# A shift filter in 32-row TensorE tiles, its gating in 1024-wide passes, and exchanges of 512 KB, in a kernel whose instruction order is written out

## Chip, cores, metric

One core of one Trainium2 chip. The metric is device microseconds of one execution. Of the many chips that were used, each comparison uses one: a changed kernel and the kernel before run in turn on the same chip. (e1 to e4 ran on one chip, e5 to e8, e17 and e18 on a second, e9 to e15 on a third, e16 on a fourth; runs of different chips are compared only by their ratios to the kernel before.) A run counts as slow, and is left out of the ratios, when it is over 1.5% above the fastest of the same kernel.

## The reference, cut

Two blocks on 2048 rows of 512 channels, in bf16. The change lies in the first.

```
k_shift = sum over t in 0..3 of k_pad[:, t:t+S, :] * shift_k[:, 3-t]     # a causal filter of 4 taps, per channel
kv = k_shift * v                                                          # "gating"
y  = irfft2(rfft2(kv padded to 2S) * rfft2(ssm_k padded to 2S))[:S]       # a long convolution per channel
out1 = q * (y + kv * ssm_D)
# ... then block B: layer norm, w1, gelu, w2, layer norm, w3 (512 to 1792), gelu, w4
```

## The kernel before: the parts that matter

Every piece of work is a numbered task; one string, ORDER, lists all of them in the order in which they are emitted. A word is a task, its engine (P TensorE, V VectorE, A ScalarE, G GpSimd, S the DMA queue on SyncE, M one merged ScalarE eviction for two tasks) and its PSUM banks. Each engine runs its own words in that order; waits between engines follow from the data. So a late task holds up all words behind it on its engine.

```python
ORDER = """
002S 023V 021P7 033V 022P 051P01 003S 052A 055P23 ...   # [cut: 791 words]
"""
    def emit(self):
        for word in ORDER.split():
            t, slots, i = self.t[int(word[:3])], [int(c) for c in word[4:]], 0
            ...                                         # [cut]
            t["fn"](word[3], t["got"].get("ps", slots))

    def shift(g, c):                     # filter of 512 rows (g) and 128 channels (c), into one bank
        s, b4 = divmod(g, 2)
        def f(e, sl):
            o = ps[:, sl[0], :]
            for i, d in enumerate((0, 1, 2, 3, -1, -2, -3)):
                j0, j1 = max(0, -d), min(3, 3 - d)
                ...                      # [cut: row block bb, offset x]
                nc.tensor.matmul(o[:, (d + j0) * P:(d + j1 + 1) * P], lhsT=kT[s][c][:, bb, x:x + P],
                                 rhs=diag[:, c, j0:j1 + 1, :].rearrange("p j x -> p (j x)"), start=(i == 0), stop=(i == 6))
        return f

    for g in range(2):                   # exchange between the two steps of a transform, 256 KB each
        for kl in range(4):
            nc.sync.dma_start(z2[sig][g:P:2, kl, :, :], z1[sig][kl:P:4, 2 * g:2 * g + 2, :, :])   # [a task ("X", sig, g, kl)]
```

The names in the profile: r_k is k, r_dg the diagonals with the taps (a per-channel product done as a matmul with a diagonal matrix), r_kv the gated product, r_x and r_y the results of a transform's first step, r_f and r_a the same data after the exchange, r_p the products of spectra, r_vs the inverse transform's first result.

Of the kernel before, what the change touches and what calls it, by code (L numbers as in the profile page):

```python
# [9 lines left out]
P = 128  # L10
# [3 lines left out]
DC = D // P  # L14
FC = F // P
NB = 8
# [15 lines left out]
002S 023V 021P7 033V 022P 051P01 003S 052A 055P23 056A 057P45 005S 025V 029V 001S 000S 024V 053P01 034G 041V 058A 047P23 049P67 048A 008S 028G 007S  # L32
027V 050A 083P50 032V 089P4 091P71 097P6 009S 084V 010S 031G 054A 042V 043A 006S 026G 030A 095P5 004S 014S 059P01 060A 061P23 038V 090V 035G 062A
093P4 015S 087P1 098V 096V 011S 036V 037A 039V 040A 085P6 092V 094V 111P23 020S 112A 064S 088V 086V 107P01 108V 109P45 110A 045G 113P67 114A 012S
103P23 105P01 066S 106A 104V 099P45 100V 101P67 102A 013S 019S 063S 340V 175P31 176V 335G 067S 018S 071P0145 073A 179P7 343V 338V 180V 072A 339V 068S
342V 119S 120S 074P2345 076A 075A 177P6 178V 115S 123P0145 124A 125V 046G 135V0 116S 126P6723 128A 127A 065S 117S 121S 129P0145 131A 130A 136V1
137P23670 139V2 016S 138V3 145V0 118S 140P 144V1 148V2 183P50 184V 069S 147V3 141A 077P0123 341V 142A 146P45671 149P 017S 337V 079A 154V0 070S 078A
153V1 122S 132P0123 134V 150M 151A 133A 143S 080P4567 155P01230 157V2 156V3 158P 336V 081A 162V0 082A 163V1 165V2 166V3 181P5 152S 185P4 344G 182V
160A 159A 161S 164P23671 167P 168A 169V 170S 189P1 186V 187P0 195P23 044A 190V 188V 332S 197P45 345G 346G 347G0 198V 196A 191P67 192A 193P01 194A
203P23 204V 205P45 199P67 200V 206A 350G1 171P10 351V 201P23 202A 229S 227S 348V 349A 356G1 353G0 352A 172P76 173P54 239P01 357V 358A 230S 231P23 240A  # L40
232A 354V 228S 362V1 363V 364A 359V0 371G 355V 331S 214S 241P67 242A 207S 372G 373V 368G1 374V0 360V 377V1 233P01 174P43 234A 369V 243P67 244A 361A
375P20 376V 213S 209S 384G 385G 365G0 378P5 379V 245P01 235P67 246A 386V 387V0 208S 397G 398G 237P23 238A 380P5 390V1 236A 370A 366V 367A 410G 210S
388P11 391P0 211S 212S 251S 392V 382P4 383A 389V 248S 252S 381A 215P2367 399V 400V0 395P1 403V1 401P00 404P4 216V 250S 405V 217A 268V0 402A 393P5 394A
396A 267V1 270V2 221P2367 223A 411G 406P4 412G 413G0 408P5 258P0167 407A 249S 222V 259V 416G1 414P40 260V 409A 423P5 417P3 415A 418A 424V 425A 427P4
428V 429A 253S 247S 261P0123 263V 447G 421P7 422A 419P6 420A 271V3 262V 224P2345 226A 225A 435P7 436V 431P6 432V 334S 255P0145 256V 443P7 333S 437A
433A 448G 449G 450G0 451P60 444V 257V 452A 218P0123 220A 219A 453G1 454P6 455V 439P7 254S 269P23450 476G 272P 477G 478G 480A0 479V1 456P60 457A 466P1
481S 274V0 273V1 275P 276V2 467A 277V3 278P 280A 440V 282V0 279A 264P0167 283V1 464P5 465A 468P4 265V 445A 284P01231 286V2 285V3 441A 287P 266V 632G
288V0 482S 483S1 469A 289V1 292V2 291V3 484P50 496P4 497A 485A 492P7 493A 290P 293P 294A 488P7 434V 633G 634G 490P6 430V 491A 494P5 281S 489A 298V0
297V1 301V2 486P4 299P01670 300V3 304V0 495A 636G0 638S 302P 487A 501P5 635V1 295A 296S 303V1 306V2 307V3 305P 308P 309A 438V 502V0 503S 498P4 310A
312V0 313V1 314P01231 315V2 316V3 317P 499V1 318V0 462P7 319V1 321V2 504S 322V3 508V 458P6 459A 509V 507S 515V 514V 505S 511V 463A 506S 512V 513V  # L50
460P5 461A 320P 323P 324M 325A 637S 470P7 311S 510V 473P6 516V 517G 500S 426V 471V0 326S 474V1 518V 522V0 519A1 327P75 523V 528G0 524A 520V 521A
328P64 529V 534A0 525V1 329P32 330P51 639S0 640P70 644P4 650P0 526V 531V1 530A 527A 535V 543G 544G 545V 549V0 546V1 645A 651A 642P6 643A 641A 646P4
647A 547P20 532V 536V 533A 556G 652P0 557G 558V 559A1 540G0 472S 548V 550P4 551V 560V0 537V1 538V 648P7 649A 653A 541V 561S 562S 542A 568G 569G 570V
571V1 539A 552P6 573S 572V0 554P4 555A 574S 654P7 553A 592P6 593V 596P5 580G 581G 597V 582G 584V0 583A1 657P4 563S0 566P6 567A 442V 564P5 565A 598V
594V 660V 661G 662V 664G0 655V0 575S1 578P3 579A 663V1 576P6 577A 608P5 609V 585S 586S 587S0 475S 588P7 589A 590P5 612P6 666S 665S 613V 667S0 591A
616P5 617V 620P7 621V 622A 604P6 610A 614V 688G 668P50 670P7 678P3 605V 680P6 671A 599V 618A 716V 669A 689G 690V 679A 692V0 694S 691V1 693S 600P7 601V
603V 602A 672P5 673A 674P3 675A 717G 718G 719V0 720V1 681A 695S1 722S 676P7 677A 624P5 625V 626A 628P6 623V 685P7 595V 606V 744V 745G 746G 696P50
708P3 709A 682P2 627V 706P3 721S 629V 631V 723S0 700P6 701A 630A 446V 747G0 749S 611V 702P1 703A 619V 683V1 684S 724P20 732P6 707A 697A 726P3 728P5
704P1 727A 615V 748V1 750S 772G 773G 774G 776A0 658V1 778S 698P4 725A 733A 730P0 656S 736P6 751S1 699A 734P4 731A 705A 710P3 713P2 752P10 729A 775V1
735A 777S 779S0 764P0 711V0 756P3 757A 753A 780P50 781A 788P4 784P3 785A 789A 754P1 782P5 783A 659S 714V1 715S 790P4 786P3 792P5 737A 738P6 686V1 791A  # L60
687S 787A 793A 797P7 794P5 760P4 761A 758P3 795V1 796S 712S 759A 607V 762P5 763A 798V1 799S 741P4 739V0 740S 765A 755A 766P5 742V1 743S 767V0 768S
769P7 770V1 771S
# [39 lines left out]
def body(ctx, tc, fx, kt, q, v, sd, w1, w2, w3, w4, out):  # L102
# [69 lines left out]
    diag = r_dg[:].rearrange("p (c j x) -> p c j x", c=DC, j=4)  # L172
# [7 lines left out]
    hbt = ct("hbt", 2, D)  # L180
    junk = {"A": ct("junka", D, dt=mybir.dt.uint8), "V": ct("junkv", D, dt=mybir.dt.uint8)}
# [57 lines left out]
    make_identity(nc, ident[:])  # L239
    ui, us = ti[0][:, 0:512], ti[1]  # L240
# [10 lines left out]
    for o, terms in enumerate((((4, 16), (2, 8), (0, 4), (1, 2), (5, 1)), ((6, 64), (7, 1)), ((3, -1024), (7, 3072)), ((3, 3072),),  # L251
                               ((5, 4), (6, 8), (0, 128), (1, 256), (2, 512), (3, 1024), (4, 2048)), ((5, 64), (0, 16), (1, 32), (7, 1)),
                               ((3, -3072), (7, 3072)), ((4, 2), (2, 1)))):
        for b, w in terms:
            pool.memset(wf[:, o, b:b + 1], float(w))
# [45 lines left out]
    add("wend", {PEc: 0.01}, lambda e, sl: None, drop=[("warm", 0)])  # L301
# [4 lines left out]

    def dg(c):
        def f(e, sl):
            for j in range(4):
                sc = sskf[:, 4 * c + j:4 * c + j + 1]  # L310
                if e == GP:
                    pool.tensor_scalar(out=diag[:, c, j, :], in0=ident[:], scalar1=sc, scalar2=0.0, op0=MUL, op1=ADD)
# [536 lines left out]
```

## Time and profile before

| | before |
|---|---|
| time, median of 3 | 213.88 us (213.87 to 214.77) |
| span of the profiled run, mean granted clock | 211.8 us, 1.00 |
| matmuls and PE busy | 2388, 197.7 us (93%) |
| VectorE, ScalarE busy | 145.5 us, 126.6 us |
| shift filter on PE | 112 matmuls, 15.3 us |
| rear, from the second half's product transform to the end | 168.4 us |

### The profile page before, as it was taken

The page shows a single profiled execution, that of the slowest core. Times are in us where ns is not written, and L with a number is a line of the kernel's source. Part 1 is how long each engine was busy: PE and PEld are TensorE (multiplying, and loading weights), DVE is VectorE, ACT ScalarE, POOL GpSimd, SP SyncE. Part 2 cuts the span into 40 slices and gives each one's busy share as a digit, 9 for nine tenths or more (in the row PEclk, how much of TensorE's full clock was granted, in tenths as well). Part 3 has the DMA queues.
Part 4 walks back from the last instruction along what each step waited for, and adds up shares of the span by engine and source line. Part 5 has one row for each costly group of instructions (what it writes and reads, how often), then busy time and mean ns, then how long its engine had stood idle before and what let it go on. Part 6 is the DMA issues. An engine that isn't in the chain of part 4 may idle for free.

```text
span 211.8 us, 5915 instructions
## 1 busy us (share of the span) xinstructions
PE 197.7 (93%) x2388; PEld 118.7 (56%) x2388; DVE 145.5 (69%) x322; ACT 126.6 (60%) x205; POOL 67.5 (32%) x171
## 2 busy tenths in 40 slices
PE   7999866998899998999999999989999999999993
PEld 5554322543375546674654784747657866864641
DVE  7699999999978999969789994627695102100421
ACT  4979899798998796672261875335622740540500
POOL 7534000765956452570003774202153200000000
PEclk9999999999999999999999999999999999999999
DMA  6999893388949952503576028470262252000111
GB/s 213 333 384 362 342 314 153 128 265 260 407 183 313 421 215 55 152 19 124 125 251 159 3 51 127 89 148 11 53 148 55 47 130 69 28 0 0 64 60 50
DMA packets 31772, 33.42 MB, mean 158 GB/s; under 512 B 22529, under 2 KB 24578, under 8 KB 31490
## 3 DMA queue, kind: packets, MB, share of 16 engines
q1 hardware_dynamic: 31746, 33.06, 49.3%
q8 instruction: 18, 0.29, 0.6%
q14 instruction: 8, 0.07, 0.1%
HBM read 13.13 MB, written 4.72 MB: 84 GB/s over the span
## 4 chain that ended last, share of the span: by engine, by line
PE 60%; ACT 14%; DMA 12%; issue 5%; SPq 4%; DVE 3%; POOL 0%; DVEq 0%; ACTq 0%
PE ps L774 20%; PE ps L786 20%; PE ps L723 6%; PE ps L694 6%; ACT r_x L265 4%; DMA r_k<-in_kt_dram 3%; ACT r_y L265 3%; DMA r_q<-in_q_dram 3%; DMA r_f<-r_x 2%; PE ps L494 2%; SPq L276 2%; PE ps L513 2%; SPq L413 2%; PE ps L421 2%; DMA dlb<-r_k 2%
## 5 line engine op out<-in xcount | busy, mean ns | idle before, releaser
L774 PE MATMUL ps<-r_dg,r_k 128*128 128x256 bf16 x448 | 51.2, 273 | 0.8 <-ACT r_vs L265 0.6
L774 PEld LDWEIGHTS <-r_k 128*128 128x128 bf16 x448 | 43.3, 98 | 8.9 <-issue 2.1
L788 DVE TENSOR_TENSOR ob<-ps,r_a 128x512 bf16<-128x512 f32 x5 | 3.5, 692 | 22.9 <-PE ps L786 21.5
L786 PE MATMUL ps<-w4s,r_kv 128*128 128x512 bf16 x84 | 19.0, 379 | 0.0
L778 ACT ACTIVATE r_f<-ps 128x512 bf16<-128x512 f32 x16 | 9.2, 595 | 15.0 <-PE ps L774 15.0
L265 ACT CAST r_x<-ps 128x1024 bf16<-128x1024 f32 x16 | 15.2, 1021 | 2.3 <-PE ps L397 2.3
L694 PE MATMUL ps<-hnT,r_v 128*128 128x256 bf16 x128 | 15.5, 273 | 1.0 <-DVE r_q L726 0.9
L778 ACT ACTIVATE r_kv<-ps 128x512 bf16<-128x512 f32 x21 | 11.7, 594 | 7.0 <-PE ps L774 7.0
L494 PE MATMUL ps<-r_p,ttab 32*32 32x512 bf16 x768 | 15.2, 378 | 0.7 <-ACT r_a L265 0.3
L723 PE MATMUL ps<-r_v,r_h 128*128 128x512 bf16 x64 | 15.5, 379 | 0.0
L450 PE MATMUL ps<-r_dg,r_k 128*128 128x256 bf16 (+3 forms) x112 | 15.3, 288 | 0.0
L778 ACT ACTIVATE r_y<-ps 128x512 bf16<-128x512 f32 x12 | 6.9, 597 | 13.9 <-PE ps L774 13.9
L786 PE MATMUL ps<-w4s,r_f 128*128 128x512 bf16 x64 | 15.1, 379 | 0.0
L694 PEld LDWEIGHTS <-r_v 128*128 128x128 bf16 x128 | 12.1, 98 | 4.8 <-issue 1.5
L265 ACT CAST r_vs<-ps 128x1024 bf16<-128x1024 f32 x11 | 10.9, 1039 | 5.8 <-PE ps L494 4.7
L265 ACT CAST r_f<-ps 128x1024 bf16<-128x1024 f32 x14 | 13.6, 1028 | 0.7 <-PE ps L421 0.7
L397 PEld LDWEIGHTS <-f 128*32 128x32 bf16 x256 | 6.9, 100 | 11.8 <-issue 6.9
L450 PEld LDWEIGHTS <-r_k 128*128 128x128 bf16 x112 | 9.3, 98 | 7.4 <-issue 2.7
L698 ACT ACTIVATE r_h<-ps 128x512 bf16<-128x512 f32 x16 | 9.1, 611 | 7.1 <-PE ps L694 7.1
L786 PEld LDWEIGHTS <-r_kv 128*128 128x128 bf16 x84 | 8.1, 98 | 9.3 <-issue 0.2
L494 PEld LDWEIGHTS <-ttab 32*32 32x32 bf16 x768 | 8.2, 88 | 7.4 <-issue 5.3
L458 DVE TENSOR_TENSOR r_kv<-ps,r_v 128x512 bf16<-128x512 f32 x16 | 10.3, 680 | 2.0 <-DMA r_v<-in_v_dram 2.0
(177 smaller groups left out, 364.8 us busy)
## 6 DMA issues: line engine op xcount, KB each, us to landing
r_x<-r_vs SPq DMA_DIRECT2D x8, 512.0 KB, 3.4
r_k<-in_kt_dram SPq DMA_DIRECT2D x8, 259.0 KB, 6.6
r_v<-in_v_dram SPq DMA_DIRECT2D x4, 512.0 KB, 6.2
r_q<-in_q_dram SPq DMA_DIRECT2D x8, 256.0 KB, 5.2
r_f<-r_x SPq DMA_DIRECT2D x8, 256.0 KB, 5.5
r_a<-r_y SPq DMA_DIRECT2D x8, 256.0 KB, 3.2
r_f<-r_y SPq DMA_DIRECT2D x8, 256.0 KB, 6.1
r_y<-r_x SPq DMA_DIRECT2D x8, 256.0 KB, 3.6
```

The lines of the kernel that those rows point to most:

```text
L265: (act.copy if e in "AM" else on[e].tensor_copy)(o, i)
L276: add(name, {SP: 0.47 if size < 400 else 0.6}, lambda e, s: nc.sync.dma_start(dst, src), deps, size=size)
L397: nc.tensor.matmul(ps[32 * j:32 * j + 32, sl[hh], :], lhsT=f1t[:, 4 * t + 2 * hp + hh, :], rhs=src(2 * b + b0), start=True, stop=True)
L450: nc.tensor.matmul(o[:, (d + j0) * P:(d + j1 + 1) * P], lhsT=kT[s][c][:, bb, x:x + P], rhs=diag[:, c, j0:j1 + 1, :].rearrange("p j x -> p ...
L458: vec.tensor_tensor(out=kvs[:, got(("K", g, 0), "kv")[0], :, c * P:(c + 1) * P], in0=ps[:, got(("K", g, c))[0], :].rearrange("p (b x) -> p ...
L494: nc.tensor.matmul(ps[c:c + 32, bk[h], :], lhsT=ttab[32 * h:32 * h + 32, 2 * kl + t, 2 if x else xx, 32 * b0:32 * b0 + 32], rhs=prs[32 * h ...
L694: nc.tensor.matmul(ps[:, sl[0], j * 256:(j + 1) * 256], lhsT=w1s[:, k, m * P:(m + 1) * P], rhs=hnT[:, k_, k, :], start=(k == 0), stop=(k = ...
L698: act.activation(h1T[:, 2 * h:2 * h + 2, 2 * p:2 * p + 2, 1 + P * s:1 + P * s + P], ps[:, got(("W", s, p, h))[0], :].rearrange("p (j b x) ...
L723: nc.tensor.matmul(ps[:, sl[0], :], lhsT=h1T[:, m, bb, x:x + P], rhs=w2s[:, m, :], start=(m == 0), stop=(m == DC - 1))
L774: nc.tensor.matmul(ps[:, sl[0], j * 256:(j + 1) * 256], lhsT=w3s[:, k, fc * P:(fc + 1) * P], rhs=lnT[:, k_, k, :], start=(k == 0), stop=(k ...
L778: act.activation(gb(gi, 2 * fp, 2), ps[:, got(("M", s, p, fp))[0], :].rearrange("p (j x) -> p j x", j=2), ACT.Gelu_apprx_tanh)
L786: nc.tensor.matmul(ps[:, sl[0], :], lhsT=gb(gi, fc)[:, 0, (b % 2) * P:(b % 2 + 1) * P], rhs=w4s[:, fc, :], start=(fc == 0), stop=(fc == FC ...
```

## The change

Its intent: of the products that a 128-row matmul with a diagonal matrix forms, all but one in 128 are by zero. With tiles of 32 rows, two row groups are to run at once into two banks, and PE needs 8.4 us (estimate in the prediction) for what took 14.8. The gating then reads a pair of banks in one pass; the diagonals shrink to 128x128 in all; exchanges are issued half as often. The order was written anew around these durations.

```diff
-ORDER = """ 002S 023V 021P7 033V 022P 051P01 003S 052A ...
+ORDER = """ 041V 003S 021P7 005S 033G 037G 031V 022P ...        # [cut: a whole new order, 776 words in all]
+    for r in range(3):                                           # four 32-row identities side by side
+        pool.tensor_tensor(out=id32[:], in0=id32[:] if r else ident[:, 0:32], in1=ident[:, 32 * r + 32:32 * r + 64], op=ADD)
-    def shift(g, c):
+    def shift(g, k):
+            for c in range(DC):
             for i, d in enumerate((0, 1, 2, 3, -1, -2, -3)):
-                nc.tensor.matmul(o[:, (d + j0) * P:(d + j1 + 1) * P], lhsT=kT[s][c][:, bb, x:x + P],
-                                 rhs=diag[:, c, j0:j1 + 1, :].rearrange("p j x -> p (j x)"), start=(i == 0), stop=(i == 6))
+                    for u in range(2):
+                        r = 32 * (2 * k + u)
+                        nc.tensor.matmul(ps[:, sl[u], :].rearrange("p (j x) -> p j x", j=4)[:, d + j0:d + j1 + 1, 32 * c:32 * c + 32],
+                                         lhsT=kT[s][c][r:r + 32, bb, x:x + P], rhs=diag[r:r + 32, c, j0:j1 + 1, :], start=(i == 0), stop=(i == 6))
-        for g in range(2):
-            for kl in range(4):
-                    nc.sync.dma_start(z2[sig][g:P:2, kl, :, :], z1[sig][kl:P:4, 2 * g:2 * g + 2, :, :])
+        for kl in range(4):
+                nc.sync.dma_start(z2[sig][:, kl, :, :], z1[sig][kl:P:4, :, :, :])
+    for i in range(4):                                           # 32 spare matmuls, placed at the very end
+        add(("fill", i), {PEc: 0.46}, fill, ...)
     # [cut: gating over two banks, one product per diagonal, the channels of k laid out anew on the host,
     #  the bit order of one table for the new exchange, dependences]
```

A filter task now has 56 matmuls and 56 weight loads and takes all four 128-channel pieces of k.

## The prediction

> **What bounds the kernel now.** I read the strip of forty slices first, to find stages with different limits, and then a table of windows cut at the stage borders.
>
> ```profile
> PE   7999866998899998999999999989999999999993
> DVE  7699999999978999969789994627695102100421
> ACT  4979899798998796672261875335622740540500
> DMA  6999893388949952503576028470262252000111
> ```
>
> One digit is 5.3 us. From 21 to 37 us (slices 4 to 6) PE has gaps (8, 6, 6), while DVE and ACT stand at 9 and the DMA engines are busy until 32 us. From slice 11 on (58 us) PE is at 9 to the last slice, but for one 8. So there are two kernels in one: a front of 43 us that transforms the data (shift filter, gating, first transforms), limited by ACT, DVE and transfers, and a rear of 165 us limited by PE. The windows say it in microseconds (columns: PE, PEld, DVE, ACT, POOL busy, clock, DMA share, GB/s):
>
> ```profile
> 8.00:16.40 8.40, 8.31 (x76) 5.09 (x72) 6.38 (x13) 7.05 (x12) 2.92 (x7) 1.00 1.01 378
> 16.40:21.50 5.10, 4.93 (x73) 2.23 (x72) 4.85 (x6) 5.10 (x7) 2.48 (x6) 1.00 0.93 363
> 21.50:28.50 7.00, 5.17 (x98) 2.02 (x97) 6.78 (x11) 6.41 (x8) 0.00 (x0) 1.00 0.88 311
> 28.50:36.00 7.50, 5.25 (x175) 2.30 (x168) 7.50 (x13) 7.50 (x8) 0.00 (x0) 1.00 0.70 264
> 150.00:180.00 30.00, 30.00 (x214) 20.78 (x213) 12.61 (x27) 11.69 (x24) 5.92 (x10) 1.00 0.36 85
> ```
>
> From 28.5 to 36 DVE and ACT have no idle time at all and PE has 2.25 us. The shift filter (L450, sixteen groups of seven matmuls, one per 512 rows and 128 channels) lies wholly in this front: eight groups between 8.1 and 16.4, then one at a time up to 43. Its rows, those of the gating (L458) and of comparable work:
>
> ```profile
> L450 PE MATMUL ps<-r_dg,r_k 128*128 128x256 bf16 (+3 forms) x112 | 15.3, 288 | 0.0
> L458 DVE TENSOR_TENSOR r_kv<-ps,r_v 128x512 bf16<-128x512 f32 x16 | 10.3, 680 | 2.0 <-DMA r_v<-in_v_dram 2.0
> L265 DVE CAST r_y<-ps 128x1024 bf16<-128x1024 f32 x6 | 7.1, 1219 | 0.6 <-PE ps L397 0.4
> L494 PE MATMUL ps<-r_p,ttab 32*32 32x512 bf16 x768 | 15.2, 378 | 0.7 <-ACT r_a L265 0.3
> L494 PEld LDWEIGHTS <-ttab 32*32 32x32 bf16 x768 | 8.2, 88 | 7.4 <-issue 5.3
> ```
>
> The chain that ended last, in order of time, shows where the front really waits:
>
> ```profile
> 4.79 7.21 DMA r_k<-in_kt_dram
> ...
> 12.36 1.28 ACT r_dg L314 x4
> ...
> 18.89 1.77 ACT r_y L265 x2
> 20.66 0.04 issue
> 20.70 1.07 ACT r_y L265
> 21.78 0.52 SPq L413
> ...
> 26.56 5.23 DMA r_f<-r_x
> ...
> 38.36 1.85 PE ps L450 x14
> 40.21 0.61 PE ps L494 x33
> ```
>
> The last piece of k lands at 12.0, ACT builds a diagonal from it, and from there the chain is ACT evictions, the SP queue (exchange issues, L413) and landings. Only 1.85 us of shift filter stand on it: 14 matmuls, so 0.925 us per group of seven.
>
> **What the Trainium skill says.** "TensorE: Matmul & The Clock Gate", LDWEIGHTS: a 32x128 weight load takes as long as a 128x128 one, the columns count. The trace has 98 ns for 128*128, 94 for 64*128, 88 for 32*32; it agrees as far as it goes and says a small tile saves nothing on the load. "TensorEngine Tiling (Array Packing)", Key Properties: a change of tiling mode drains the array. The trace has it: each lone filter group is preceded by 0.42 us of idle weight load. "VectorE: DVE Perf Modes", Side-by-side: in mode 1x one element per cycle at 0.96 GHz plus about 150 cycles. For 512 columns that is 0.69 (measured 0.68), for 1024 1.22 (measured 1.219). "DMA: Bandwidth & Descriptors", Anatomy of one DMA: some 2.0 us fixed plus bytes over 436 GB/s, so 3.2 us for 512 KB; the eight 512 KB exchanges of the inverse transform land after 3.4 us in the median, the 256 KB ones after 3.2 to 6.1, which is queueing and not size.
>
> **The change part by part.**
> Filter. Before: 16 x 0.925 = 14.8 us. After: eight tasks of 56 matmuls, each two 32-row groups side by side. A row group streams 4 x (128+96+64+32+96+64+32) = 2048 columns, exactly what one old group streams for a quarter of the output of a task pair; two run at once. Fourteen matmuls of 512 columns take 3.02 us in the chain, so 2048 columns take 0.86. The other limit is instructions: L494 gets 64 matmuls with their loads through in 1.08 (chain of waits), 17 ns a pair, so 56 need 0.95. Small moving sizes (32 columns) must expose some loads; I choose 1.05, the order's own table says 0.86. 8 x 1.05 = 8.4: PE sheds 6.4 us.
> Gating. 16 x 0.68 = 10.9 becomes 8 x 1.22 = 9.8: DVE sheds 1.1.
> Diagonals. Sixteen scalings (DVE 8 x 0.249, POOL 4 x 0.406, ACT 4 x 0.39, the ACT four on the chain for 1.28) become four small products, estimated at 0.25 on DVE and 0.5 on POOL, none on ACT.
> Exchanges. 32 issues of about 0.6 become 16: 9.6 us off the SP queue. The bytes (8 MB) stay, and a transfer now waits for all eight evictions instead of four.
> Order. Loads: all of k's first half and all of the filter's spectrum input come first, v after them. The activation table for GELU (1.28 + 0.20 on ACT) moves from 43 us to about 24. 32 spare matmuls were put after the last real one, beside the last add and store: no cost.
>
> What of it counts:
> 1. To the last eviction before the second exchange (21.76 now). 1.84 MB must land before the filter starts; the strip moves 213 GB/s in the first slice and 333 in the second, which gives 7.4, plus 1.4 from last byte to use (2.9 MB took until 12.0): 8.8, and diagonals until 9.4. Two tasks of 1.05: 11.5. Then ACT, never idle again: two evictions, two tables, five evictions, 2.0 + 1.9 + 4.9 plus the first transform's 0.6: 20.9. Gain 0.8, not the 3.2 us that PE sheds here (8 x 0.925 less 4 x 1.05), because ACT takes over.
> 2. To the end of the first convolution (41.6). DVE does 16 products at 0.61 and about 3.7 us of other work either way, and ACT now has the table load in it (+1.5) and its 0.8 head start: products start at 27.3 again, DVE sheds 0.7. PE's shorter tasks here only make its gaps wider. Gain 0.6 in place of 0.8.
> 3. Behind it: two filter groups (1.85) stand between the convolution and the next transform; in the new order one task stands behind the first transform step. 1.85 less 1.05: gain 0.8. ACT is spared the 1.5 us of table load at 43 and has one 0.8 us normalization instead: gain 0.7, as ACT is full from 44 to 60.
> 4. Rear. The same matmuls; in the order I count six more changes of tiling mode than before, at about 0.14 each (a lone 8-matmul transform takes 0.57 against 0.43 of streaming): loss 0.8. PE's idle there is some 5 us; a fresh order may recover 1 and I credit that, with little to go on.
> Sum: 0.6 + 0.8 + 0.7 - 0.8 + 1.0 = 2.3. 213.9 - 2.3 = 211.6; I lean a little further, to 211.3, since loads and exchanges with half the issues can only relieve the queue.
>
> **The rivals.**
> PE is the bound throughout, so all 6.4 us come back: 207.5. For it: 93% busy. Against: the gaps at 22 to 36 us, with ACT and DVE at 7.50 of 7.50.
> Small tiles run badly (weight loads of 128 columns exposed, 1.6 us a task): the filter then costs 12.8, PE sheds 2, and the first two tasks before ACT's chain cost 1.1 more: 213. For it: the load is no shorter for 32 rows. Against: the 17 ns per pair of L494.
> Coarse exchanges: waiting for all eight evictions delays the first transfer (19.99 now) by some 1.5 us and pushes 2 MB at once behind the v loads; if stage 2 starts later by that, 213.5 to 214.5. For it: DMA at 0.88 to 1.01 there. Against: the consumer needs both halves anyway, so only the last landing counts.
>
> **Range and chances.** The parts sum to 1 to 4 us gained; a fresh order shifts waits by 2 either way. 80% range 208.0 to 214.3. Over 2% faster means below 209.6, which needs most of the PE saving: 0.27. Slower than 218.2 needs tiles twice as bad as feared: 0.05. Within 2%: 0.68.
>
> **What would show it.** A filter task at 0.95 to 1.15 us from its first to the next task's first matmul, PE busy down by about 6 without the spare ones; gating at 1.22; no diagonal on ACT; ACT without a gap from about 12 to 40 us; the first convolution's end near 41. Wrong: if that end comes before 39 (then the front was PE's or the queue's after all), if a filter task takes over 1.3, or if the rear from the second transform to the last matmul is not within 2 us of 165.

## More of the kernel before

Besides the lines in the prediction, three of TensorE's own timeline (start, duration, then what; neighbours of one kind are joined):

```profile
8.07 4.53 PE L450 MATMUL ps<-r_dg,r_k 128*128 128x512 bf16 x35
...
13.69 2.80 PE L450 MATMUL ps<-r_dg,r_k 128*128 128x512 bf16 x21
16.41 1.91 PE L397 MATMUL ps<-r_kv,f 128*32 128x512 bf16 x32
```

Five filter tasks run from 8.07 us, one after the other, each on the 128 channels whose piece of k has come; three more follow once the last piece and its diagonal are there. At 16.41 the transform of the gated product begins. Below, the start of this transform ("product transform"), the first matmul of its second step behind the second exchange ("second step"), and the start of the product transform of the second half of the rows serve as milestones.

## The result, and the profile after

224.41 us in the median (223.77 to 225.59, four runs) against 214.32 (213.87 to 215.47): slower by 4.7%, ratio 1.0469 (1.0405 to 1.0533). Here and below a ratio is the mean time of one kernel's fast runs over that of the other's of the same rounds, so not quite the ratio of the medians. The span of the profiled run is 222.5 us against 211.8, its mean granted clock 0.939 against 1.000.

The strips of the changed kernel (a slice is 5.6 us; the last line is the granted clock in tenths, which is all nines before):

```profile
PE   5959498789979999999999999989999999999996
DVE  4856968677799899998698698618735730220321
ACT  3964959767999968857234496144731540518000
PEclk9996955558999999999999999999999999999999
```

The front has gaps on all three engines where before it had DVE and ACT at 9, and the clock is down to half from 28 to 52 us and for a stretch before (17.5 to 20.9). The stretches between the milestones (9.0, 18.09, 24.9, 35.36 and 51.6 us; columns as in the prediction):

```profile
9.00:18.09 9.09, 6.76 (x253) 4.95 (x248) 5.97 (x12) 5.89 (x7) 4.17 (x12) 0.97 0.90 332
18.09:24.90 6.81, 5.75 (x84) 2.38 (x81) 5.41 (x7) 5.38 (x7) 0.75 (x2) 0.79 0.69 212
24.90:35.36 10.46, 7.05 (x178) 4.11 (x177) 8.38 (x12) 7.99 (x8) 1.61 (x3) 0.64 0.88 311
35.36:51.60 16.24, 13.86 (x360) 6.10 (x359) 11.59 (x17) 12.27 (x12) 3.88 (x9) 0.50 0.24 95
```

In no stretch is ACT or DVE full now; in the last, the inverse second steps and what lies between them, PE is busy 85% of the time at a clock of 0.50. The rows of the groups:

```profile
L452 PE MATMUL ps<-r_dg,r_k 32*128 32x96 bf16 (+3 forms) x448 | 11.1, 213 | 4.4 <-issue 2.3 <-ACT r_f L275 2.1
L463 DVE TENSOR_TENSOR r_kv<-ps,r_v 128x1024 bf16<-128x1024 f32 x8 | 9.7, 1222 | 5.8 <-PE ps L452 4.0 <-issue 1.8
L500 PE MATMUL ps<-r_p,ttab 32*32 32x512 bf16 x768 | 18.3, 459 | 1.8 <-ACT r_a L275 0.9 <-DVE r_a L267 0.6 <-DVE r_p L488 0.3
```

The filter is at 11.1 us on PE and a gating pass at 1222 ns, but the filter has 4.4 us of idle time before its instructions, 2.3 of it put down to "issue", time in which nothing that the profile shows was waited for. L500 (L494 before) has 459 ns a matmul in place of 378 in the mean, as a part of them runs at half clock. The chain that ended last, in order of time, then TensorE's timeline at the same place and ScalarE's behind it:

```profile
14.03 2.33 issue
...
25.80 1.78 ACT r_f L275
27.62 3.35 PE ps L452 x85
```

```profile
13.37 0.66 PE L452 MATMUL ps<-r_dg,r_k 32*128 32x128 bf16 x27
16.36 1.80 PE L452 MATMUL ps<-r_dg,r_k 32*128 32x32 bf16 x85 [2.33 <-issue]
```

```profile
19.18 1.93 ACT L267 CAST r_y<-ps 128x1024 bf16<-128x1024 f32 x2 [3.16 <-PE ps L398]
```

Before, the chain in this place went through loads, ACT's evictions and the DMA queue; now it goes through the filter, and through a stop of 2.33 us in the middle of a filter task, between its 27th and 28th matmul, with no other engine involved. ScalarE then waits 3.16 us for the product transform behind this task. Two more losses follow: a merged eviction of two bank pairs at once (L275, 1.9 us), for which filter tasks wait that need one of the pairs, and these two tasks, at half clock, ahead of the second step.

The milestones, read from TensorE's timelines (us from the span's start; the last column is span less the one before):

| | product transform | its end | second step | inverse begins | second half begins | rear |
|---|---|---|---|---|---|---|
| before | 16.41 | 20.59 | 25.43 | 28.49 | 43.38 | 168.4 |
| after | 18.09 | 23.22 | 30.88 | 35.36 | 51.62 | 170.8 |

Of the 10.7 us in the span, 8.2 are lost ahead of the second half and 2.4 behind. Two of these 2.4 lie in the product transform of the second half, which takes 7.5 us from its first to its last matmul instead of 5.5, as a filter task has been moved into it. This milestone cuts the two kernels at different work, though: before, two filter groups (1.9 us) stand just ahead of it. Counted from the end of the first convolution instead (41.60 and 51.69 us), 10.1 us are lost ahead of it and only 0.6 behind.

### The profile page after: what moved, and what is told of

Same layout as the page of the kernel before. It is cut to its first block, busy times and chain, and to the rows that moved or that the text cites. A ratio compares the mean times of both kernels' runs of the same rounds, so it can differ in the third digit from the quotient of the medians.

```text
span 222.5 us, 6576 instructions
## 1 busy us (share of the span) xinstructions
PE 203.3 (91%) x2743; PEld 123.8 (56%) x2756; DVE 146.3 (66%) x315; ACT 124.6 (56%) x195; POOL 63.5 (29%) x175
## 4 chain that ended last, share of the span: by engine, by line
PE 69%; ACT 11%; DVE 9%; issue 6%; DMA 4%; SPq 0%; POOL 0%; ACTq 0%; DVEq 0%
PE ps L780 20%; PE ps L792 19%; PE ps L500 7%; PE ps L700 5%; PE ps L398 5%; PE ps L452 4%; PE ps L729 4%; ACT r_y L267 3%; PE ps L421 2%; DMA r_x<-r_vs 2%; ACT r_vs L275 2%; PE ps L519 2%; DVE r_q L732 2%; DMA r_h<-in_fx_dram 1%; DVE r_v L621 1%
## 5 line engine op out<-in xcount | busy, mean ns | idle before, releaser
L780 PEld LDWEIGHTS <-r_k 128*128 128x128 bf16 x448 | 43.3, 98 | 8.4 <-issue 2.6
L500 PE MATMUL ps<-r_p,ttab 32*32 32x512 bf16 x768 | 18.3, 459 | 1.8 <-ACT r_a L275 0.9
L792 PE MATMUL ps<-w4s,r_kv 128*128 128x512 bf16 x80 | 18.7, 379 | 0.2
L267 ACT CAST r_x<-ps 128x1024 bf16<-128x1024 f32 x15 | 14.3, 1023 | 4.5 <-PE ps L398 4.5
L729 PE MATMUL ps<-r_v,r_h 128*128 128x512 bf16 x59 | 14.9, 379 | 1.0 <-ACT r_h L704 0.7
L500 PEld LDWEIGHTS <-ttab 32*32 32x32 bf16 x768 | 9.4, 91 | 10.7 <-issue 7.2
L398 PEld LDWEIGHTS <-f 128*32 128x32 bf16 x256 | 7.4, 107 | 14.1 <-issue 10.7
L452 PE MATMUL ps<-r_dg,r_k 32*128 32x96 bf16 (+3 forms) x448 | 11.1, 213 | 4.4 <-issue 2.3
L792 PE MATMUL ps<-w4s,r_f 128*128 128x512 bf16 x63 | 14.9, 379 | 0.1
L452 PEld LDWEIGHTS <-r_k 32*128 32x128 bf16 x448 | 10.5, 105 | 7.2 <-issue 6.3
L700 PEld LDWEIGHTS <-r_v 128*128 128x128 bf16 x128 | 12.1, 98 | 4.1 <-issue 2.3
L752 POOL TENSOR_TENSOR xrr<-xrr,mhalf 128x2 f32<-128x2 f32 x8 | 7.1, 883 | 24.3 <-DVE xrr L598 24.0
L267 ACT CAST r_vs<-ps 128x1024 bf16<-128x1024 f32 x10 | 9.7, 1014 | 7.2 <-PE ps L500 5.6
L463 DVE TENSOR_TENSOR r_kv<-ps,r_v 128x1024 bf16<-128x1024 f32 x8 | 9.7, 1222 | 5.8 <-PE ps L452 4.0
L794 DVE TENSOR_TENSOR r_kv<-ps,r_a 128x512 bf16<-128x512 f32 x3 | 2.1, 691 | 16.9 <-PE ps L792 16.9
```

Of the source, the lines that this page charges most:

```text
L267: (act.copy if e in "AM" else on[e].tensor_copy)(o, i)
L398: nc.tensor.matmul(ps[32 * j:32 * j + 32, sl[hh], :], lhsT=f1t[:, 4 * t + 2 * hp + hh, :], rhs=src(2 * b + b0), start=True, stop=True)
L452: nc.tensor.matmul(ps[:, sl[u], :].rearrange("p (j x) -> p j x", j=4)[:, d + j0:d + j1 + 1, 32 * c:32 * c + 32], lhsT=kT[s][c][r:r + 32, b ...
L463: vec.tensor_tensor(out=lay(kvs[:, got(("K", g, 0), "kv")[0]]), in0=pair(got(("K", g, k))).rearrange("p r (b x) -> p r b x", b=4), in1=lay ...
L500: nc.tensor.matmul(ps[c:c + 32, bk[h], :], lhsT=ttab[32 * h:32 * h + 32, 2 * kl + t, 2 if x else xx, 32 * b0:32 * b0 + 32], rhs=prs[32 * h ...
L700: nc.tensor.matmul(ps[:, sl[0], j * 256:(j + 1) * 256], lhsT=w1s[:, k, m * P:(m + 1) * P], rhs=hnT[:, k_, k, :], start=(k == 0), stop=(k = ...
```

## The experiments

Eighteen kernels ran, all with correct results. Two of them told nothing (e9, e11), as said there. The table has the medians of all runs, the slow ones included (one each of e8, e13, e14 and e17, two of e15); the ratio is of fast runs alone, to the kernel before, on the same chip (e1 to e4 ran on one chip, e5 to e8, e17 and e18 on a second, e9 to e15 on a third, e16 on a fourth).

| run | us | ratio | second half begins at, us |
|---|---|---|---|
| e1 new order, 128-row filter | 225.31 | 1.0522 (1.0466 to 1.0578) | 52.94 |
| e2 changed, first merge split | 222.8 | 1.0392 (1.0321 to 1.0463) | 50.65 |
| e3 before, 512 KB exchanges | 214.48 | 1.0017 (0.9948 to 1.0086) | 45.31 |
| e4 e1 and e2 together | 222.46 | 1.0383 (1.0319 to 1.0447) | 49.42 |
| e5 changed, no merges | 221.1 | 1.0321 (1.0258 to 1.0383) | 49.47 |
| e6 e5, PE kept busy | 222.2 | 1.0412 (1.0335 to 1.0489) | 48.35 |
| e7 e5, front order moved | 222.4 | 1.0405 (1.0341 to 1.0469) | 50.60 |
| e8 before, 32-row filter | 220.54 | 1.0283 (1.0194 to 1.0373) | 48.63 |
| e10 before, filter in 64-wide pieces | 216.31 | 1.0074 (1.0022 to 1.0126) | 46.68 |
| e12 before, merges split | 213.83 | 0.9966 (0.9919 to 1.0013) | 44.64 |
| e13 e8 with 128-row tiles | 222.5 | 1.0389 (1.0292 to 1.0485) | 54.11 |
| e14 e8, idle stretch filled | 220.26 | 1.0303 (1.0217 to 1.0389) | 49.63 |
| e15 e14, last diagonal sooner | 219.73 | 1.0214 (0.9909 to 1.0518) | 49.50 |
| e16 e15, queues laid anew | 219.23 | 1.0233 (1.0122 to 1.0344) | 47.47 |
| e17 e16 with 64-row tiles | 215.86 | 1.0026 (0.9962 to 1.0091) | 46.67 |
| e18 changed, 64-row tiles | 217.64 | 1.0171 (1.0109 to 1.0233) | 44.74 |

### e1 to e4: which part

My first theory was that the new order was at fault with its merged evictions, and the rivals were the small tiles and the coarse exchanges. The edits: e1 puts the old matmuls into the new tasks, two 128-channel groups into the two banks; e2 has one word of the order changed; e3 issues the second of two old exchanges for both; e4 is e1 and e2.

```diff
 # e1
-            for c in range(DC):
-                for i, d in ...:  for u in range(2): r = 32 * (2 * k + u); matmul(..., lhsT=kT[s][c][r:r + 32, ...])
+            for u in range(2):
+                c, o = 2 * k + u, ps[:, sl[u], :]
+                for i, d in ...:  matmul(o[...], lhsT=kT[s][c][:, ...])          # and the old diagonals
 # e2
-079M
+079A
 # e3, in the kernel before
-                    nc.sync.dma_start(z2[sig][g:P:2, kl, :, :], z1[sig][kl:P:4, 2 * g:2 * g + 2, :, :])
+                    if second of the two: nc.sync.dma_start(z2[sig][:, kl, :, :], z1[sig][kl:P:4, :, :, :])
```

> The changed kernel with its filter put back to 128-row tiles (14 matmuls a task in place of 56; full diagonals), order, 1024-wide gating and 512 KB exchanges kept. Theory (idle PE halves its clock; the small tiles starve PE of instructions): no PE gap of 2.3 us near 14 us, clock 1.0 until about 26; the 2.1 us wait behind the merged eviction stays, so the clock may fall from 28; filter task 1.85 us; 217 to 222 us. Rival (small tiles themselves count as too little activity): clock 1.0 to the end, 216 or less. Rival (512 KB exchanges are to blame): second transform of the product starts 4 us or more later than before, 220 or more.

> The changed kernel with one merged eviction (2048 wide, two bank pairs) done as two of 1024; nothing else. Theory: the gap near 14 us and the half clock around 18 to 21 stay; the 2.1 us PE wait at 25.6 is gone, the clock does not fall at 28, 215 to 219 us. Rival (small tiles): the clock falls again between 25 and 35 although the wait is gone, 222 or more.

> The kernel before with only the exchanges made coarse: each pair of 256 KB transfers is one of 512 KB, issued where the later of the two stood. Rival (coarse exchanges): 216 to 220 us, front longer by 2 us or more, whatever the clock. Theory: 213 to 215.5, clock 1.0.

> Both e1 and e2: 128-row filter and the split eviction in the changed kernel. Theory: no PE gap over 1.5 us in 14 to 28, clock 1.0 throughout, 213 to 216.5 us. Rival (coarse exchanges or the new order as such): still 219 or more with clock 1.0.

e3 clears the coarse exchanges of the 4.7%: they cost nothing that three rounds can see (its interval leaves room for 0.9%). e1 and e4 misled me for a while. With the old filter the new order is just as slow, so the small tiles seemed innocent. But the new order puts the filter late, counting on its being short: in e4 the filter tasks start at 10.07, take 0.9 us for each 128 channels, and the product transform starts at 19.02, later still than in the changed kernel (18.09). And neither e1 nor e4 has the stop. So I read it that two losses of like size had changed places; e18 fits that. e2 loses the wait for the merged eviction but keeps a stop of 2.6 us in the filter, and its clock falls to half again from 32.8 us, as its rival had said.

### e5 to e8: merges, clock, front order, filter alone

e5 splits all four merged evictions. e6 adds four spare 512-wide matmuls ahead of each later second step and inverse step, so that the clock holds. e7 moves one load and two transform tasks of the front ahead of what stood before them, and the table load for GELU behind the first convolution, where the order before had it. e8 is the kernel before with the 32-row filter, its gating and its diagonals, in the old order; the tasks stand in places of old ones, and the last two pieces of k and v were exchanged.

```diff
 # e5
-079M 122M 142M 300M
+079A 122A 142A 300A
 # e6, in the second step and in the first of each group of inverse steps
+                keep(sl[0], 4)      # nc.tensor.matmul(ps[:, bank, :], lhsT=ident[:], rhs=ftab[...], start=True, stop=True), four times
 # e7
-003S 021P7 005S ... 004S ... 091P670 051A 093P01 ... 055P23 056A 057P45 ... 052A 
+003S 021P7 004S 005S ... 055P23 091P670 051A 057P45 093P01 ... 056A ... 160A 052A
 # e8, in the kernel before: shift, gating, diagonals of the changed kernel, and
-083P50 032V 089P4 091P71 097P6 009S ... 006S 026G 030A
+032V 006S ... 009S 026G 030G 083P50 089P4 091P71 097P6
```

> The changed kernel with all four merged evictions (2048 wide) done as two of 1024; nothing else. Merged-eviction theory: the PE waits behind L275 (2.1, 1.5, 0.9 us in the changed kernel) vanish and 3 to 5 us come back: 218 to 221 us. Rival (only the half clock and the early order count): within 1 us of the run that split one of them (222.8).

> As the run without merged evictions, plus ten groups of four spare 128x512 matmuls put in front of second transform steps and inverse steps, into the bank that the step then overwrites: about 9 us more PE work, in PE's waits. Half-clock theory: clock 1.0 from about 25 us on, the first convolution ends 2 us or more earlier and the time is 1.5 to 4 us below the run without merged evictions. Rival (the half clock is a symptom, PE is not the bound there): same time or up to 4 us slower.

> As the run without merged evictions, with three orders undone: two pieces of the filter spectrum loaded first again, the last first-step transform of it ahead of the filter, and the GELU table loaded behind the first convolution again. Early-order theory: first eviction 1 us, last eviction before the second exchange 1.5 to 2.5 us earlier, 2 to 4 us faster than without them: 215 to 218 us. Rival: under 1 us.

> The kernel before with the filter alone changed: 32-row tiles, 56 matmuls a task, compact diagonals on DVE and POOL, gating in 1024-wide passes where the two banks are neighbours; old order, 256 KB exchanges (one piece of k loaded earlier, one of v later). If the filter change is good by itself: 210.5 to 213.5 us, clock 1.0. If it starves PE of instructions (a PE gap of 1.5 us or more with no releaser near 14 us) or lowers the clock by itself: 215 to 220 with the clock below 0.98.

e5 gains about 3 us (1.0321 against 1.0469, in different calls). e6 holds the clock at full from 21.8 us on, and the time does not fall, though its second half begins 1.1 us sooner. As the spare matmuls take PE time themselves, this does not clear the half clock. How much it cost in the changed kernel itself stays open; its stretch of inverse steps took 16.3 us, 14.3 in e5, 13.7 in e6. e7 has the stop too (3.1 us) and gains nothing. e8 is the first run that shows a loss from the filter and what comes with it (gating, diagonals, tasks in pairs): 6 us, in the old order, with the old exchanges. TensorE's timeline of e8:

```profile
10.74 2.19 PE L455 MATMUL ps<-r_dg,r_k 32*128 32x128 bf16 x98 [2.24 <-POOL r_dg L311]
...
16.75 2.77 PE L455 MATMUL ps<-r_dg,r_k 32*128 32x32 bf16 x85 [1.03 <-issue]
```

It shows two candidates: a wait of 2.24 us, since each new task needs the last piece of k and its diagonal, and another stop without a releaser. From 12.1 to 22.4 us the clock was at half.

### e9 to e12: two empty runs, a density, the merges of before

e9 and e11 altered the list of dependences of the filter tasks. That list had only served to make the order: nothing in emitting a task reads it, and the instructions came out the same. e9 is the kernel before once more (1.0019, 0.9969 to 1.0070) and e11 is e4 once more (222.74 us; 1.0374). As repeats they show how far one program scatters: the two profiled spans of the kernel before differ by 0.3 us, and its second half began at 43.4 and 44.3 us. The theory that they were meant to test was neither shown nor refuted by them.

```diff
 # e9, in the kernel before
-[("Lk", s, c), ("dg", c)] + ...
+[(n, s, i) if n == "Lk" else (n, i) for n in ("Lk", "dg") for i in range(DC)] + ...
 # e10, in the kernel before
+                w = 64 if i else 4 * P
+                for h in range((j1 - j0 + 1) * P // w):
-                nc.tensor.matmul(o[:, (d + j0) * P:(d + j1 + 1) * P], ...)
+                    nc.tensor.matmul(o[:, (d + j0) * P + w * h:(d + j0) * P + w * h + w], ...)
 # e11, in e4
-for c in range(DC)
+for c in (2 * k, 2 * k + 1)
 # e12, in the kernel before
-150M 324M
+150A 324A
```

> The kernel before, its order, its 128-row filter; the only edit: each filter task now waits for all four pieces of k and all four diagonals, as the tasks of the changed kernel must, and not for its own piece alone. Theory (the new tasks mix all channel chunks, so the last of four loads holds all of them): the first filter task starts near 10.7 us instead of 8.1, the first transform of the product (L397 on r_kv, 16.4 us before) starts near 19 us, and the time is 216.5 to 219.5. Rival (instruction supply and the half clock after it are what e8 lost, the wait is filled by other work): 213.5 to 214.8, nothing changes.

> The kernel before, its order, its waits, 128-row tiles; the filter's matmuls except the 512-wide ones cut into 64-wide ones: 25 weight loads and matmuls a task instead of 7, 200 in the eight tasks of the first half of the batch, near the 224 of the small tiles. If the number of TensorE instructions in this stretch is itself what costs (supply of instructions): an idle stretch of PE with no releaser of 1 us or more between 9 and 17 us, perhaps half clock after it, and 216 to 219. If it costs only because the small tiles start late and then come in one lump: no such idle stretch, and 213.5 to 215.5.

> e4 (the changed order with 128-row filter and split first merged eviction, 222.46 us) with one edit: each filter task waits for its own two pieces of k alone. Theory (in the new order the place of the tasks is fixed by the order, and the order as a whole is late): 221.5 to 223, the first transform of the product near 19 us as in e4. Rival (the wait for all four pieces is what the new order loses too): 217 to 220, that transform near 17 us.

> The kernel before with its two merged 2048-wide ScalarE evictions (L273) split into two 1024-wide ones each. No merge in the changed kernel was worth about 3 us for four merges (e5). If merging costs wherever it stands: 212 to 213.3. If the merges of before stand where nothing waits long (one wait of 1.1 us, L421 on r_vs L273): 213.3 to 214.8, the same.

e10 has 25 matmuls in a task instead of 7, so some 200 in the front, yet spread over the time that the 128-row tiles take: no stop. In time (216.3 us) it lies at the lower end of the first expectation, in the trace with the second. So this number of them, spread out, costs 0.7% (0.2 to 1.3), without a stop; what the 0.7% are was not looked into. e12: splitting the two merges of before is worth nothing that shows (interval 0.9919 to 1.0013). With e5 this fits a merge that costs only where something waits for its banks, which was not tested further.

### e13 to e15: the wait, and the clock behind it

e13 has e8's places, pairs and waits, with the old 128-row tiles and diagonals. e14 is e8 with nine spare 512-wide matmuls in the idle stretch. e15 makes the last diagonal on VectorE.

```diff
 # e13, in e8
-            for c in range(DC): ... for u in range(2): r = 32 * (2 * k + u) ...
+            for u in range(2): c, o = 2 * k + u, ps[:, sl[u], :] ...          # 128-row, old diagonals, 030A
 # e14, in e8
+            if (g, k) == (0, 0):
+                for i in range(9):
+                    nc.tensor.matmul(ps[:, sl[0], :], lhsT=ident[:], rhs=fxs[0][:, 2, :], start=True, stop=True)
 # e15, in e14
-054A 042V 043A 009S 026G 030G
+054A 009S 026V 030V 042V 043A
```

> e8 (old order, filter tasks in pairs of banks at the same places, waiting for the last piece of k) with the old 128-row tiles and old diagonals in place of the small ones: the wait alone. If the wait for the last piece is what e8 lost: first long stretch of filter near 11 us, first transform of the product near 19.3 us as in e8 (19.45), no half clock needed for it, 218 to 221. If it was the small tiles (their instructions, the idle stretch without releaser, the half clock): that transform at 17.5 us or sooner and 214 to 216.5.

> e8 with nine spare 128x512 matmuls ahead of the first filter task, about 2 us of PE work in the stretch where PE sat idle for 2.24 us. If the half clock of 13.9 to 24 us is a cause there (every matmul of the filter's second half and of the first transform of the product runs at half rate): clock full in that stretch, the transform 17.3 to 18.3 us, its 64 matmuls in 4.2 us instead of 5.4, and 215.5 to 218. If the half clock is a symptom, as in e6: clock full, time 219.5 to 221.

> e14 with the last diagonal made on VectorE ahead of its table work instead of on GpSimd (0.86 us there, against 0.25): the filter's long stretch starts 0.5 to 0.9 us sooner than in e14, and if the front is the chain that sets the end, the time is 0.5 to 1 us under e14's; if something else (the second exchange) sets it, the same as e14 within 0.4 us.

e13: waiting for the last piece costs by itself (1.0389, above what was expected), the long stretch of filter starts at 12.68 us, the product transform at 21.3; the old diagonals, made late on ScalarE, make this wait 3.2 us, longer than that of e8. So in old places the small tiles seem to make good part of the wait, though e13 is no clean measure of it. e14 was a surprise: the product transform starts at 16.50, as early as before, and the time is still 220. The loss had only moved behind it. (e15: its interval is wide; it differs from e14 by less than that.) Where it moved to is in VectorE's queue. VectorE's line of the sine table's argument, in the kernel before, then in e14 with the gating pass that precedes it:

```profile
13.99 0.68 DVE L352 TENSOR_SCALAR r_a<-r_a 128x1024 int32<-128x1024 int32 x1
```

```profile
15.23 1.23 DVE L471 TENSOR_TENSOR r_kv<-ps,r_v 128x1024 bf16<-128x1024 f32 x1 [0.44 <-PE ps L458]
16.37 0.68 DVE L347 TENSOR_SCALAR r_a<-r_a 128x1024 int32<-128x1024 int32 x1
```

The coarse gating comes later and in larger pieces, the table's argument waits behind it in the queue, and ScalarE, which needs it for the table, starts the product's evictions at 18.75 instead of 17.08.

### e16: queues laid anew

Both table arguments go ahead of the gating, both sines ahead of two evictions, and two pairs of tasks get banks for which no transform waits.

```diff
-060A 061P23 038V 090V 035G 062A ... 036V 037A 039V 040A
+061P23 038V 035G 036V 039V 037A 040A 060A 090V 062A
-    RUN = ({3: (0, (5, 4)), 1: (1, (1, 6))}, ..., {2: (0, (3, 7)), 1: (1, (6, 7))}, ...)     # place: (k, banks)
+    RUN = ({3: (0, (5, 4)), 1: (1, (7, 6))}, ..., {2: (0, (7, 6)), 1: (1, (7, 6))}, ...)
```

> e15 with three moves in the order (the arguments of the sine tables on VectorE and the sines on ScalarE ahead of the gating and of the last two evictions of the filter transform, into their idle stretches) and two filter tasks in other banks, so that no transform waits for a gating pass over their banks. If the loss of e14 and e15 is the queues behind the coarse gating: ScalarE's evictions of the product start near 17 us, the 64 matmuls of its transform take 4.2 to 4.8 us, the second exchange's first matmul (L416 on r_a) comes at 25.5 to 26.5 us instead of 28.4, and the time is 214.5 to 217.5. If it is the small tiles in another way (the half clock behind 27 us): that matmul comes sooner, and the time stays at 218.5 to 220.5.

The time, 219.2 us, and a second step that came little sooner (27.82 against 28.38) fit the second expectation. Its reason, the half clock, was there (27.9 to 31.3 and 41.5 to 51.8 us) and is not refuted, but something else came first. The table's sines were early now, as meant; TensorE stood still:

```profile
14.59 1.81 PE L458 MATMUL ps<-r_dg,r_k 32*128 32x64 bf16 x94 [0.69 <-issue]
...
20.51 1.90 PE L392 MATMUL ps<-r_kv,f 128*32 128x512 bf16 x30 [1.65 <-issue]
```

The stop had grown a twin, this time in the middle of the product's transform (L392), which has no part in the change at all. Counting TensorE's recorded instructions (matmuls, weight loads and the few waits on record) from the start of each trace gives the pattern. Every large stop without a releaser in the first 24 us begins after number 448, 449, 704 or 705, whatever instruction that is:

| kernel | number 193 starts | number 450 starts | idle before it | 16 KB instruction transfer ends |
|---|---|---|---|---|
| before | 11.24 | 21.54 | none | 15.59 |
| e10 | 9.50 | 14.64 | 0.08 | 13.17 |
| e16 | 10.63 | 14.59 (449) | 0.69 | 13.16 |
| e8 | 10.96 | 16.75 | 1.03 | 15.42 |
| after | 10.88 | 16.36 | 2.33 | 14.86 |
| e7 | 11.36 | 17.30 | 3.1 | 15.94 |

In e16 number 706 starts at 20.51 after the second stop, the next transfer ended at 19.25. The stops of e2, e5 and e6 (2.57, 2.41 and 2.15 us), not in the table, also end with number 450. The trace has a DMA queue that the page calls "instruction". In the changed kernel, in the stretch from 13.8 to 14.9 us, it moved one packet, and in the whole run 21 (name of the queue; packets, MB, share of 16 engines):

```profile
q8 instruction: 1, 0.02, 5.6%
```

```profile
q8 instruction: 21, 0.34, 0.6%
```

0.34 MB in 21 is 16 KB each. The profile does not say for which engine they are. But in all twenty traces their count is within one of TensorE's recorded instructions divided by 256 (18 for 18.7 before, 21 for 21.5 after, 19 for 19.6 in e17), so they are taken to be TensorE's. In every stop of the table TensorE goes on 1.3 to 1.5 us after such a transfer ends (after: 14.86 and 16.36), and where number 450 comes later than that by itself, there is no stop. The transfers end 2.5 to 4.7 us after number 193 (in the second stop of e16, number 449) has started; in the changed kernel the DMA engines were over 90% busy with data meanwhile. So 256 instructions that TensorE runs through in less than some 4 to 6 us leave it empty-handed here (an estimate: the sums of these two spans of time). One pair of small filter tasks is 224 instructions in 2.26 us.

### e17 and e18: half the instructions

64-row tiles test it: two row groups fill the same two banks, each matmul is twice as wide, and there are half as many. A task then needs two pieces of k.

```diff
-            for c in range(DC):
+            for c in (2 * k, 2 * k + 1):
                 for i, d in enumerate((0, 1, 2, 3, -1, -2, -3)):
                     for u in range(2):
-                        r = 32 * (2 * k + u)
-                        nc.tensor.matmul(ps[:, sl[u], :]...[:, d + j0:d + j1 + 1, 32 * c:32 * c + 32], lhsT=kT[s][c][r:r + 32, bb, x:x + P], rhs=diag[r:r + 32, ...])
+                        r = 64 * u
+                        nc.tensor.matmul(ps[:, sl[u], :]...[:, d + j0:d + j1 + 1, 64 * (c % 2):64 * (c % 2) + 64], lhsT=kT[s][c][r:r + 64, bb, x:x + P], rhs=diag[r:r + 64, ...])
 # and diagonals of 64 columns, the channels of k and the taps laid out to match, the gating's view of v
```

> e16 with 64-row filter tiles: half the filter's instructions, two diagonals' worth more to make (128x256 instead of 128x128). If instruction supply is what held e16 (219.2 us): no idle stretch without a releaser over 0.3 us between 13 and 21 us, the product's transform done at 20.9 to 21.5 us instead of 22.4, and 215.5 to 218. If the coarse pairs, their late gating and the late second exchange are the whole loss: idle stretches gone, their time taken by waits for VectorE and ScalarE, and 218.5 to 220.

> The changed kernel with 64-row filter tiles, nothing else. Its idle stretch of 2.3 us at 14.0 us should go or shrink under 0.7 us if the supply of instructions makes it, whatever the time does. On the time: if that stretch is on the path, 221 to 222.8 instead of 224.4; if the order behind it (late exchange, merged evictions, the filter tasks behind the convolution) sets the time anyway, 223.5 to 225.

TensorE in e17, whose first filter tasks start as in e16 (10.26 and 10.31):

```profile
16.32 4.18 PE L391 MATMUL ps<-r_kv,f 128*32 128x512 bf16 x64 [0.28 <-DVE r_kv L470]
```

Both stops are gone, the transform takes its 4.18 us as before, and the time is that of the kernel before: 1.0026 against 1.0233. But the stops' 2.3 us do not come through whole. In their place TensorE waits for an exchange:

```profile
22.41 0.83 PE L415 MATMUL ps<-r_f,ftab 64*32 64x512 bf16 x16 [1.91 <-DMA r_f<-r_x]
```

So the second step comes only 0.4 us sooner than in e16, and the second half 0.8. Another 1.5 us come in the second half's product transform (5.3 us for 6.8), which e16 runs at half clock to 51.8 us and e17 at full clock from 46.6 on. The two profiled spans are 1.8 us apart, the ratios some 4 us. In the changed kernel (e18), with nothing else altered, the second pair of filter tasks and what follows:

```profile
12.29 1.95 PE L451 MATMUL ps<-r_dg,r_k 64*128 64x256 bf16 x56
14.18 2.13 PE L397 MATMUL ps<-r_kv,f 128*32 128x512 bf16 x26
16.47 2.33 PE L397 MATMUL ps<-r_kv,f 128*32 128x512 bf16 x38 [0.17 <-issue]
...
23.30 3.60 PE L451 MATMUL ps<-r_dg,r_k 64*128 64x256 bf16 x56 [2.06 <-ACT r_f L274]
26.82 1.06 PE L420 MATMUL ps<-r_a,ftab 64*32 64x512 bf16 x16
```

A trace of the stop is left (0.17 us, at number 450). The product transform starts at 14.18, which is 3.9 us sooner than in the changed kernel and 2.2 sooner than before. The time falls to 217.64, under the 221 to 222.8 that I had expected: 1.0171 against 1.0469, some 6.4 us (difference of the ratios times 214.3). The PE clock, at half from 28 to 52 us in the changed kernel, is at half from 21.7 to 28.6 us only, and the stretch from the second step to the second half takes 17.9 us instead of 20.7. Then the order takes part of it back: from the product transform's end to the second step it needs 8.0 us, where the kernel before needs 4.8, as the lines show: the filter tasks wait 2.06 us for a merged eviction and then stand for 3.6 us at half clock ahead of the second step. e18 without its merges, and with these two tasks behind the second step, is the version that I would have run next; whether it beats the kernel before stays open. None of the eighteen is shown to.

## Why the prediction was wrong

**Sizes of the parts.** A pair of filter tasks takes 2.26 us where TensorE is fed (1.13 a task, 1.05 predicted, and 1.73 if the two row groups did not overlap: an estimate, two times 2048 columns at 3.02 us for 14 matmuls of 512), a gating pass 1.222 (1.22), a diagonal 0.29 on VectorE in the page's mean and 0.40 on GpSimd (0.25 and 0.5), and none is on ScalarE. PE busy rose from 197.7 to 203.3 instead of falling by 6: some 1.9 are the spare matmuls, and the half clock lengthened what was left (L500 alone 18.3 us for 15.2). The other terms were right and of no use.

**Step 1 failed, in "Then ACT, never idle again", and with it the head start of 0.8 us.** The first two tasks took what was predicted (2.26 us for 2.1), but began at 10.2 and not at 9.4. The second pair is not in the sum: it was to be done while ScalarE was busy. For that the step took it that instructions come as fast as the array can take them, and had its rate from L494, 64 pairs in 1.08 us. Such a burst is 128 instructions, shorter than a block of 256: it shows the array's rate, not that of the supply. The supply gives some 256 in 4 to 6 us in this stretch (the estimate above), and the second pair of tasks stood still for 2.33 us. So the product transform began at 18.09, ScalarE stood idle for 3.16 us ahead of it, and the last eviction ahead of the second exchange ended at 24.9 (predicted 20.9). Of these 4.0 us, 1.0 is the late start and the size of the first pair; the idle time accounts for the rest. e18 fits this: with the supply mended, ScalarE's longest wait there is 0.34 us and this eviction ends at 20.56 us (19.55 and 1.01 on ScalarE). It does not prove the rest of the step, since its first task, which needs two pieces of k and not four, also begins at the predicted 9.4.

**Step 2 failed too, by itself.** It predicted the first convolution's end near 41; it came at 51.7, and at 44.8 in e18. I added up the work of VectorE and ScalarE and held the queues to be full; I did not look at which task stands ahead of which. In the new order a merged eviction, the table load for GELU and two filter tasks stand ahead of the second step. e5 puts some 3 us on the merges in the changed kernel; e7 moves the table load back, with two other moves, and gains nothing. How the rest divides, and what the half clock has in it, was not tested.

**Step 3 and 4.** From the end of the first convolution to the end of the next product transform the kernel before needs 7.3 us and the changed one 7.4: the gain of 0.8 for moving a filter task, and that of 0.7 on ScalarE, cannot be found. Behind this transform the changed kernel loses 0.5 us (163.4 for 162.9), where I had a loss of 0.8 and a credit of 1.0, given "with little to go on". e18 has the same rear (170.7), so this small part is the order's and not the supply's. What it is was not tested. Of my signs of being wrong, two came. Filter tasks took over 1.3 us: the third with the stop in it, and those at half clock 1.7 to 1.9. And from the second transform to the last real matmul it took 167.2 us instead of 165 within 2, but 1.2 of them are the moved task.

**Two lines misread.** From slice 11 on the PE strip has two 8s before the last slice, not one. And the 32*32 weight loads (88 ns) have a quarter of the columns of the 128*128 ones (98 ns), so they speak against "the columns count"; only the comparison with 64*128 (94 ns) agrees. Neither changed the sum.

**The rivals.** "PE is the bound": false, PE has more idle time now. "Coarse exchanges": not the cause of 4.7%, by e3; the small cost that this rival named (213.5 to 214.5) lies within the noise of e3 (214.48). "Small tiles run badly" was nearest, but its reason, exposed weight loads, was wrong, as the tiles run at the predicted rate until the block ends; and it had 213 us. No rival had a shortage of instructions in it, and the half clock that came with the idle time was not thought of at all. The 5% given to "slower" rested on tiles twice as bad as feared, which was the wrong question.

**What is settled and what is not.** Settled by the numbering and by e17 and e18: the stops come from the supply of TensorE's instructions and go when the filter has half as many. Shown: 64-row tiles bring back some 4 us in the old order (1.0233 to 1.0026, on two chips) and some 6 in the new one. Not shown: that all of this is the length of the stops. In the traces a part of it lies where the clock is full in place of half, and no run separates the two. (In e18 a part may also be that the first task needs two pieces of k instead of four: it starts 0.8 us sooner. In e17 it does not.) Settled by e10: such a number of instructions, spread over the time of the large tiles, makes no stop. Settled by e3: the exchanges are not the 4.7%. Open: what orders an instruction transfer, and whether the data transfers beside it delay it; the cost of the half clock in the changed kernel; and the rest of 1.7% that e18 still has over the kernel before, of which the lines name the places but no run took them away.

## What to carry to other kernels

Before cutting matmuls small, count the instructions of the stretch, weight loads too, and set them against the rate at which a stretch of several hundred of them was seen to run, not against the rate of a short burst. If an engine stops with nothing released in the middle of a loop, number its instructions from the start of the program in two kernels: the same number twice points to supply, not data. And where a new order is written around a shorter task, a test that puts the long task back has to be read with care, since it may lose as much for a different reason, as e1 and e4 seem to have done.

## What the Trainium skill lacked or had wrong

- "Trainium Architecture — The Big Picture", The software stack: it has instructions of 64 bytes and their streams brought to each engine at load. The traces have 18 (before) and 21 (after) further transfers of 16 KB during the run, which is 256 instructions of that size, and stops at numbers that differ by 256 (448 and 704 in e16).
- "Runtime: NRT & Kernel Launch", Instruction fetch mechanics, does have the refill during a run, in blocks of 16 KiB or 256 instructions, but takes its cost as mostly hidden. Here it is not where two small filter tasks run in 2.26 us: TensorE goes on 1.3 to 1.5 us after the end of a transfer, with stops of up to 3.1 us (e7). In the kernel before, where number 450 comes at 21.54 us, 6 us after the transfer's end, it is hidden.
- "TensorEngine Tiling (Array Packing)", Instruction Overhead: about 60 cycles a matmul, however small, and the advice not to take the tiling from a dimension that is small already. The runs agree with the advice (the 32-row tiles have moving sizes of 32 to 128); for the sizes, 112 pairs in two row groups took 2.26 us, 20 ns each. The section lacks that two such tasks outrun the supply of instructions.
